# A fused attention and gated-MLP block: the start-up stage regrouped, with stacks copied from on-chip tiles, early row maxima, and token stores last

## Chip, cores and metric

The kernel runs on one core of a Trainium2 chip. The metric is the device time of one execution in microseconds (us); the median of several runs is given. All arithmetic is in float32, with matmul operands split into a high and a low part ("hi" and "lo") and multiplied in three products, so that precision is kept.

## What is computed

```python
# S = 2048 tokens, D = 512, H = 32 heads of 16, gated MLP of width 2 x 896
xn  = layernorm(x)
qkv = xn @ wqkv
p   = softmax(q @ k.T * 16 ** -0.5)          # per head, 2048 x 2048
A   = concat_heads(p @ v) @ wo
z   = gelu(xn @ w_in); z1, z2 = z[:, :896], layernorm(z[:, 896:])
B   = (z1 * (w_sp @ z2 + b_sp[:, None])) @ w_out
out = x + A + B
```

## The kernel before

Heads are taken in 16 pairs. For a pair p the "stacks" `qst[p % 2]` and `kst[p % 2]` hold, for each of its two heads at partitions 0 and 64, 48 rows: the 16 rows of q (or k) three times, as hi or lo parts in the order that makes one 48-row matmul give all three products. Two more rows carry the negated row maxima for the softmax (in `qst`) and ones (in `kst`).

The program has two stages.

The **prologue** (the body of `tc.manual_schedule`, L972 to L1022) is an order written out by hand. The tokens come in four groups g of 512. Per group: `norm_x` (statistics on VectorE, the scaling on ScalarE, L305), `turn_x` (16 TensorE transposes into four PSUM banks, each split into hi and lo by ScalarE and VectorE through `split`, L327 and L229), `qk_first` (24 matmuls by the weights `w0` of the first four pairs' q and k, L389, with a split and the stores to the DRAM scratch `qscr[0]`, `kscr[0]`), `load_stacks` (reads the stacks of pair 0 back from that scratch, L785) and `v_tile` (12 matmuls for one of the 16 tiles of v; `EARLY` = 4 of them are made here, L441). PSUM has four tiles, `dps` and three `sl`, taken in turn by `bank`. At the end the 16 transposed token tiles `xnT[g, c]` are put out to `xscr` (L1012) through `store`, which in the prologue issues on GpSimd's queue (L153).

The **steady stage** (the loop from L1229) writes out the rest of the program, with a planner that keeps a planned time for each engine and chooses, slot after slot, what TensorE does next. Its order of slots is fixed when the program is built. The slots are S (`scores`, L1076: one 512 x 128 piece of scores for two heads, followed by an exponential on ScalarE), M (`maxima`, L1093: the same product the other way round, followed by a maximum over 512 keys on VectorE, L806), V (`values`, L1170: eight exponentials times v, 32 matmuls in a burst), D (`dense_slot`, L1142: two matmuls of everything else, in the order v_rest, qk_rest, z2_all, z1_all, spatial, mlp_out, attn_out) and fillers (L1155). A "round" ends with a V burst; there are 128 of them. The first score needs the maxima of 512 queries over all keys: 16 M slots, then `max_fin` (L811), which writes the maxima to the scratch `mscr` and reads them back into the two extra rows of `qst`; both transfers go through SyncE's queue (SP), as do the loads of the next weights (`begin`, L249, under `weight`, L271). The planner lets M slots begin at planned time `FIRST` after the prologue (L1109).

In the built program each transfer on SP waits at its issue, among other things, for the one eight transfers earlier on SP to have landed.

Of the kernel before, what the change touches and what calls it, by code (L numbers as in the profile page):

```python
# [16 lines left out]
P = 128  # L17
# [13 lines left out]
GC = 0.7978845608028654  # L31
RING = 19
EARLY = 4
FIRST = 7.0
DEEP = 4
LEAD = 30
AGE = 6.0
# [14 lines left out]
def fused_block(ctx, tc, x, wqkv, wo, w_in, w_spT, b_sp, w_out, out):  # L52
# [96 lines left out]
    def store(dst, src, us=0.3):  # L149
        if steady:  # L150
            after(us, move, dst, src)
        else:
            nc.gpsimd.dma_start(raw(dst), raw(src))  # L153
# [63 lines left out]
    def t512(nm):  # L217
        return big.tile([P, 512], F32, tag="t512", name=nm, bufs=4)

    def hilo(nm):  # L220
        return big.tile([P, 2, 512], F32R, tag="hilo", name=nm, bufs=3)

    turns = [0]

    def bank():
        turns[0] += 1
        return (dps, *sl)[turns[0] % 4][:, 0, :]

    def split(dst_h, dst_l, src):  # L229
        act(dst_h, src, AF.Copy)  # L230
# [64 lines left out]
    def load_x(g):  # L295
        xt = [at_.tile([P, 2, D], F32, tag="pf", name=f"x{g}_{i}", bufs=PF) for i in (0, 2)]
        for i in range(len(xt)):
            k = 4 // len(xt)
            t = 4 * g + k * i
            rows = x[t * P:(t + k) * P, :]  # L300
            move(xt[i], rows if k == 1 else rows.rearrange("(a p) d -> p a d", p=P))
            for j in range(k):
                xs[g, k * i + j] = xt[i] if k == 1 else xt[i][:, j, :]

    def norm_x(g, parts=1):  # L305


        mv = sm.tile([P, 4, 2], F32, tag="mv", name=f"mv{g}", bufs=2)
        rs = sm.tile([P, 2, 4], F32, tag="rs", name=f"rs{g}", bufs=2)
        k = 4 // parts  # L310
        for a in range(parts):
            tiles = range(a * k, (a + 1) * k)
            sl = slice(a * k, (a + 1) * k)
            for i in tiles:
                st = sm.tile([P, 6], F32, tag="bst", name=f"bst{g}_{i}", bufs=4)
                nc.vector.bn_stats(st, xs[g, i])
                nc.vector.bn_aggr(mv[:, i, :], st)
            yield
            nc.scalar.activation(rs[:, 0, sl], mv[:, sl, 1], AF.Sqrt, bias=epst)
            nc.vector.reciprocal(rs[:, 0, sl], rs[:, 0, sl])  # L320
            nc.vector.scalar_tensor_tensor(rs[:, 1, sl], mv[:, sl, 0], -1.0, rs[:, 0, sl], ALU.mult, ALU.mult)
            for i in tiles:
                if i % 4 == 2:
                    yield
                nc.scalar.activation(xs[g, i], xs[g, i], AF.Identity, bias=rs[:, 1, i:i + 1], scale=rs[:, 0, i:i + 1])

    def turn_x(g):  # L327
        for c in range(ND):
            pt = bank()
            for i in range(4):  # L330
                nc.tensor.transpose(pt[:, i * P:(i + 1) * P], xs[g, i][:, c * P:(c + 1) * P], ident)
            t = piece(f"xnT{g}_{c}")
            split(t[:, 0, :], t[:, 1, :], pt)
            xnT[g, c] = t
# [43 lines left out]
    def qk_store(scr, order, hl, sl_, first=False):  # L378
        put = move if first else store
        r = 1 if order[0] == order[1] else 0  # L380
        put(scr[:, r:r + 2, sl_], hl)
        put(scr[:, 2 - 2 * r, sl_], hl[:, 0, :])

    def qk_weights(m, a):
        return f"wqk{m}_{a}", wqkv[:, a * D + m * P: a * D + (m + 1) * P], D, ND

    QK = ((0, 1, 0), (0, 0, 1))

    def qk_first(g, w):  # L389
        for a in range(2):  # L390
            acc = bank()
            for c in range(ND):
                t = xnT[g, c]
                mm3(acc, w[a][:, 0, c * P:(c + 1) * P], w[a][:, 1, c * P:(c + 1) * P], t[:, 0, :], t[:, 1, :], c == 0, c == ND - 1)
            hl = hilo(f"qkhl0_{a}_{g}")
            split(hl[:, 0, :], hl[:, 1, :], acc)
            qk_store((qscr, kscr)[a][0], QK[a], hl, slice(g * 512, (g + 1) * 512), True)
            yield

    def qk_out(m, g, a):  # L400
# [40 lines left out]
    def v_tile(t, ws):  # L441
        acc = bank()
        sl_ = slice((t % 4) * P, (t % 4 + 1) * P)
        for c in range(ND):
            xt = xnT[t // 4, c]
            mm3(acc, xt[:, 0, sl_], xt[:, 1, sl_], ws[c][:, 0, :], ws[c][:, 1, :], c == 0, c == ND - 1)
        act(vhead[:, t, :, :DH], acc.rearrange("p (h d) -> p h d", d=DH), AF.Copy)
# [337 lines left out]
    def load_stacks(p, cols=slice(0, S)):  # L785
        m, r = p // 4, (p % 4) * 2
        q, k = qst[p % 2], kst[p % 2]
        sl = [slice((r + j) * DH, (r + j + 1) * DH) for j in range(2)]
        for j in range(2):
            for i, (t, scr) in enumerate(((q, qscr), (k, kscr))):  # L790
                args = t[64 * j:64 * j + KS, cols], scr[m][sl[j], :, cols]
                if p and 2 * j + i:
                    later(2 * j + i, move, *args)
                else:
                    move(*args)

    NSTEP = NP * 64
    mmax = {}
    maxready = {}

    def max_red(i, k, ready):
        g, (t, kc) = i // 16, divmod(i % 16, 4)
        yield "D", td(1024)
        if i % 16 == 0:
            mmax[g] = at_.tile([P, 2, 4, 4], F32, tag="mm", name=f"mm{g}", bufs=2)
        nc.vector.tensor_reduce(mmax[g][:, :, t, kc], sl[k], AX.X, ALU.max)  # L806
        free_slot(k)
        if i % 16 == 15:
            yield from max_fin(g)
# [161 lines left out]
    with tc.manual_schedule(engines=engines):  # L971
        load_x(0)  # L972
        w0 = [piece(f"wqk0_{a}") for a in range(2)]
        w0r = [begin(*qk_weights(0, a), early=w0[a]) for a in range(2)]
        load_x(1)
        ones = t512("ones")
        nc.vector.memset(ones[0:32, 0:P], 1.0)
        wv, wvr = [], []
# [15 lines left out]
        init_rows(0)  # L994
        for r, t in zip(wvr, wv):
            end(r, t, True)
        norm = norm_x(1, 2)
        for g in range(NG):
            for _ in qk_first(g, w0):
                if g == 0:  # L1000
                    next(norm, 0)
            load_stacks(0, slice(g * 512, (g + 1) * 512))
            for t in range(EARLY * g // NG, EARLY * (g + 1) // NG):
                v_tile(t, wv)
            if g + 1 < NG:
                for _ in norm:
                    pass
                turn_x(g + 1)
                if g + 2 < NG:
                    norm = norm_x(g + 2)  # L1010
                    next(norm)
        for g in range(NG):  # L1012
            for c in range(ND):
                store(xscr[g][c], xnT[g, c])
        steady.append(True)
        braw = t512("braw")[0:16, 0:P]
        bhl = hilo("bhl")[0:16, :, 0:P]
        move(braw, b_sp)
        nc.vector.tensor_copy(bhl[:, 0, :], braw)
        nc.vector.tensor_sub(bhl[:, 1, :], braw, bhl[:, 0, :].bitcast(F32))  # L1020
        for a in range(2):
            move(bsplit[a:a + 1, :], bhl[:, a, :])  # L1022
        T.update(P=0.0, A=0.0, D=0.0, G=0.0)
        room["big"] = RING - 16 + EARLY
        prepare(wq, [((m, a), *qk_weights(m, a)) for m in (1, 2, 3) for a in range(2)])
# [16 lines left out]
        wrote = [0] * 3  # L1042
        stpos = {}
        mode = "R"
        n_st = n_mx = n_pv = 0

        def take(what, n=1):
            nonlocal pe, seen
# [44 lines left out]
        def maxima():  # L1093
            nonlocal n_mx
            p, r = divmod(n_mx, 64)
            tt, kc = divmod(r, 4)
            turn_to("R")
            k = take("m")
            for j in range(2):
                rows = slice(64 * j, 64 * j + KS)  # L1100
                nc.tensor.matmul(sl[k][:, j, :], qst[p % 2][rows, tt * P:(tt + 1) * P], kst[p % 2][rows, kc * 512:(kc + 1) * 512], start=True, stop=True)  # L1101
            T["P"] += SLOT
            spawn(max_red(n_mx, k, 0), 1, T["P"] + 0.22)
            n_mx += 1
# [7 lines left out]
        def has_dense(t):  # L1112
            nonlocal blocked, swap, hold, seen
            while not slots:
                if blocked > t or dfree[0] > t or hold or not queue:
                    return False
                it = next(queue[0], None)
                if it is None:
                    queue.pop(0)
                elif it[0] == "t":  # L1120
                    slots.extend(it[1])
                elif it[0] == "w":
                    blocked = t + it[1]
                elif it[0] == "s":
                    swap = True
                elif it[0] == "q":
                    hold = spent > 11 and n_pv < N
                elif it[0] == "e":
                    dfree[0] = FAR
                    held[0] = len(it[1])  # L1130
                    for g in it[1]:
                        spawn(g, 0, T["P"] + 0.25)
            if swap and seen < lastd:
                nc.tensor.drain()
                seen = pe
                T["P"] += DRAIN
            swap = False
            return True
# [156 lines left out]
```

## Time and profile before

| | us |
|---|---|
| timed runs | 1898.93, 1893.89, 1898.62 (median 1898.62) |
| profiled execution, its own time | 1894.84 |
| span of its trace | 1892.8 |
| TensorE busy in the span | 1829.1 (97%) |
| VectorE busy | 1443.6 (76%) |
| ScalarE busy | 1225.3 (65%) |
| GpSimd busy | 659.0 (35%) |

The profiled execution is one run; its own time is 2.04 us above the span of its trace. In the rows of the timeline the first column is the start and the second the length in us; a bracket at the end gives the engine's idle time before the row and what ended it. PEld rows are weight loads, which lie beside the matmuls.

### The profile page before, as it was taken

What the parts mean: (1) busy time and instruction counts of PE and PEld (TensorE: products, weight loads), DVE (VectorE), ACT (ScalarE), POOL (GpSimd) and SP (SyncE); (2) the same over time, 40 slices, a digit from 0 to 9 for tenths busy, and PEclk for the clock granted to TensorE, in tenths of its full rate; (3) what the DMA queues carried; (4) which work ended last, traced back from release to release, by engine and by line L of the source; (5) the groups of instructions that cost most, each with busy time, mean ns of one, the idle gap of its engine ahead of it and who ended that gap; (6) DMA issues with size and microseconds to landing.
All of it is one profiled execution on the core that took longest, in us unless ns stands there. A gap on an engine that the chain in (4) does not pass through costs nothing.

```text
span 1892.8 us, 38090 instructions
## 1 busy us (share of the span) xinstructions
PE 1829.1 (97%) x14830; PEld 1113.3 (59%) x14830; DVE 1443.6 (76%) x1677; ACT 1225.3 (65%) x1338; POOL 659.0 (35%) x757
## 2 busy tenths in 40 slices
PE   6899999999999999999999999999999999999998
PEld 5666566565555566566655666566565655555654
DVE  5578878888886878777877777787687778777883
ACT  4247777888775777666656666666566666565655
POOL 2302142787887777700161206000612030002110
PEclk9999999999998999999999999999999999999999
DMA  9506572444555354645677557463957666366342
GB/s 328 207 3 190 191 239 86 115 119 117 155 156 164 118 135 130 147 134 135 168 204 177 166 136 219 132 145 101 229 155 172 165 184 161 103 149 185 115 127 93
DMA packets 234732, 291.46 MB, mean 154 GB/s; under 512 B 36008, under 2 KB 136040, under 8 KB 231672
## 3 DMA queue, kind: packets, MB, share of 16 engines
q1 hardware_dynamic: 230328, 279.00, 54.2%
q0 software_dynamic: 4224, 10.04, 1.5%
q8 instruction: 116, 1.90, 0.5%
q14 instruction: 64, 0.52, 0.1%
HBM read 186.98 MB, written 101.98 MB: 153 GB/s over the span
## 4 chain that ended last, share of the span: by engine, by line
PE 83%; DMA 6%; DVE 4%; POOL 3%; issue 2%; ACT 2%; SPq 0%; DVEq 0%; POOLq 0%; ACTq 0%
PE dps L1146 33%; PE sl L1184 22%; PE sl L1087 13%; PE sl L1101 12%; DVE mm L806 3%; DMA zs<-z2scr 2%; PE dps L1160 1%; POOL wsp L282 1%; ACT pf L69 1%; DMA wsp_11r<-in_w_spT 1%; DMA qst<-qscr 1%; DMA wqk<-in_wqkv 1%; DMA xnT__6256<-xscr 1%; POOL wsp L280 1%; DMA hscr<-hhl 0%
## 5 line engine op out<-in xcount | busy, mean ns | idle before, releaser
L806 DVE TENSOR_REDUCE mm<-sl 128x2 f32<-128x1024 f32 x1024 | 1226.4, 1223 | 190.6 <-PE sl L1101 186.4
L69 ACT ACTIVATE pf<-sl 128x1024 f32<-128x1024 f32 x1024 | 1043.3, 1026 | 369.9 <-PE sl L1087 330.9
L1184 PE MATMUL sl<-pf,vall 128*32 128x512 f32 x4096 | 467.8, 597 | 1.3 <-ACT pf L69 1.3
L1146 PE MATMUL dps<-wsp,zs 64*128 64x512 f32 x2688 | 449.2, 396 | 8.6 <-DMA zs<-z2scr 8.5
L1087 PE MATMUL sl<-qst,kst 50*128 50x512 f32 x2048 | 445.2, 421 | 12.2 <-DVE mm L806 2.9
L1101 PE MATMUL sl<-kst,qst 48*128 48x512 f32 x2048 | 432.6, 409 | 6.4 <-DVE mm L806 3.2
L1087 PEld LDWEIGHTS sl<-qst,kst 50*128 50x128 f32 x2048 | 200.5, 185 | 221.7 <-issue 85.7
L1146 PEld LDWEIGHTS dps<-wsp,zs 64*128 64x128 f32 x2688 | 272.8, 189 | 51.4 <-DMA zs<-z2scr 8.1
L1184 PEld LDWEIGHTS sl<-pf,vall 128*32 128x32 f32 x4096 | 120.3, 110 | 272.5 <-issue 240.8
L1101 PEld LDWEIGHTS sl<-kst,qst 48*128 48x128 f32 x2048 | 200.4, 186 | 110.8 <-ACT pf L69 54.1
L1204 DVE TENSOR_TENSOR e<-sl,e 128x512 f32<-128x512 f32 x64 | 44.1, 690 | 165.4 <-PE sl L1184 134.5
L718 POOL TENSOR_TENSOR hhl<-z1i,hhl 128x512 fp32r<-128x512 f32 x28 | 35.5, 1284 | 353.0 <-ACT hhl L69 303.3
L69 ACT ACTIVATE e<-sl 128x512 f32<-128x512 f32 x64 | 38.4, 600 | 172.9 <-PE sl L1184 158.3
L1146 PE MATMUL dps<-w,xt 64*128 64x448 f32 x768 | 110.8, 369 | 2.3 <-ACT z L69 0.4
L1146 PE MATMUL dps<-wout,hp 64*128 64x512 f32 x672 | 111.4, 392 | 0.0
L1146 PEld LDWEIGHTS dps<-w,xt 64*128 64x128 f32 x768 | 73.7, 186 | 17.4 <-issue 8.0
L1146 PEld LDWEIGHTS dps<-wout,hp 64*128 64x128 f32 x672 | 65.5, 187 | 8.9
L418 POOL TENSOR_TENSOR qkhl<-qr,qkhl 128x512 fp32r<-128x512 f32 x24 | 30.4, 1285 | 114.9 <-ACT qkhl L69 114.8
L853 POOL TENSOR_TENSOR ob<-ob 128x512 f32<-128x512 f32 (+1 forms) x16 | 20.6, 1286 | 141.1 <-DMA ob<-rscr 108.6
L849 POOL TENSOR_TENSOR ob<-ob 128x512 f32<-128x512 f32 (+1 forms) x16 | 20.5, 1284 | 129.4 <-DMA ob<-escr 129.4
L1146 PE MATMUL dps<-xnT,wqk 64*128 64x512 f32 x288 | 47.4, 396 | 1.1 <-ACT vall L69 0.4
L1160 PE MATMUL dps<-brow,zeror 64*128 64x512 f32 x258 | 46.5, 402 | 1.7 <-ACT z L69 1.4
(277 smaller groups left out, 1595.0 us busy)
## 6 DMA issues: line engine op xcount, KB each, us to landing
zs<-z2scr SPq DMA_DIRECT2D x192, 256.0 KB
escr<-e SPq DMA_DIRECT2D x60, 256.0 KB
hscr<-hhl SPq DMA_DIRECT2D x28, 512.0 KB
qst<-qscr SPq DMA_DIRECT2D x30, 384.0 KB
kst<-kscr SPq DMA_DIRECT2D x30, 384.0 KB
xscr<-xnT POOLq DMA_DIRECT2D x16, 512.0 KB, 4.6
qscr<-qkhl SPq DMA_DIRECT2D x16, 512.0 KB
kscr<-qkhl SPq DMA_DIRECT2D x16, 512.0 KB
```

What stands on the lines that cost most here:

```text
L69: return nc.scalar.activation(out, in_, func, **kw)
L418: nc.gpsimd.tensor_sub(hl[:, 1, :], raw_, hl[:, 0, :].bitcast(F32))
L718: nc.gpsimd.tensor_sub(hl[:, 1, :], z1, hl[:, 0, :].bitcast(F32))
L806: nc.vector.tensor_reduce(mmax[g][:, :, t, kc], sl[k], AX.X, ALU.max)
L849: nc.gpsimd.tensor_add(both_[rows, 0, :], both_[rows, 0, :], both_[rows, 1, :])
L853: nc.gpsimd.tensor_mul(both_[rows, 0, :], both_[rows, 0, :], both_[rows, 1, :])
L1087: nc.tensor.matmul(sl[k][:, j, :], kst[p % 2][rows, kt * P:(kt + 1) * P], qst[p % 2][rows, c * 512:(c + 1) * 512], start=True, stop=True)
L1101: nc.tensor.matmul(sl[k][:, j, :], qst[p % 2][rows, tt * P:(tt + 1) * P], kst[p % 2][rows, kc * 512:(kc + 1) * 512], start=True, stop=True)
L1146: nc.tensor.matmul(dps[:, bank, :w], lhs, rhs, start=go, stop=stop)
L1160: nc.tensor.matmul(dps[:, bank, :], zeror[r:r + 64], brow[r:r + 64], start=not begun, stop=not begun)
L1184: nc.tensor.matmul(sl[k][cols:cols + VW, 0, :], vpack(kt + r, 2 * p + j), pf[:, j * 512:(j + 1) * 512], start=n == n_pv, stop=n == n_pv + ...
L1204: nc.vector.tensor_add(e, sl[k][:, 0, :], e)
```

## The change

The changed prologue does five things.

- Tokens are normed and turned a group ahead: group 1 is normed and turned before the projections of group 0, and group g + 2 beside those of group g.
- `qk_first` copies the stacks of pair 0 straight from the split tile with six transfers of 16 rows for each of q (on SP) and k (on GpSimd's queue); `load_stacks(0, ...)` is gone. The scratch stores stay.
- `first_maxima(kc)` makes the first 512 queries' maxima over one quarter of the keys, four M products with their four reductions, after `qk_first` of the following group. Twelve of the first sixteen M products are thus in the prologue; the loop begins with `n_mx` = 12, and the first sixteen go by quarters of the keys.
- The 16 token stores go out through `move`, that is on SP, after everything else of the prologue; the loads and splits of `b_sp` come early.
- The loop's M slots may begin at planned time 3.0 (it was 7.0), and the D queue isn't held at its "q" marks until all tiles of v are made.

```diff
-FIRST = 7.0
+FIRST = 3.0
...
+    def turn4():
+        turns[0] += 1
+        return turns[0] % 4
+
     def bank():
-        turns[0] += 1
-        return (dps, *sl)[turns[0] % 4][:, 0, :]
+        return (dps, *sl)[turn4()][:, 0, :]
...
+    mmax = {}
     QK = ((0, 1, 0), (0, 0, 1))
+    PARTS = QK
+
+    def first_maxima(kc):
+
+        for t in range(4):
+            acc = (dps, *sl)[turn4()]
+            for j in range(2):
+                rows = slice(64 * j, 64 * j + KS)
+                nc.tensor.matmul(acc[:, j, :], qst[0][rows, t * P:(t + 1) * P], kst[0][rows, kc * 512:(kc + 1) * 512], start=True, stop=True)
+            if 0 not in mmax:
+                mmax[0] = at_.tile([P, 2, 4, 4], F32, tag="mm", name="mm0", bufs=2)
+            nc.vector.tensor_reduce(mmax[0][:, :, t, kc], acc, AX.X, ALU.max)
...
             split(hl[:, 0, :], hl[:, 1, :], acc)
-            qk_store((qscr, kscr)[a][0], QK[a], hl, slice(g * 512, (g + 1) * 512), True)
+            cols = slice(g * 512, (g + 1) * 512)
+            put = (nc.sync, nc.gpsimd)[a]
+            for j in range(2):
+                for i, part in enumerate(PARTS[a]):
+                    row = 64 * j + i * DH
+                    put.dma_start((qst, kst)[a][0][row:row + DH, cols].bitcast(F32), hl[j * DH:(j + 1) * DH, part, :].bitcast(F32))
+            qk_store((qscr, kscr)[a][0], QK[a], hl, cols, True)
             yield
...
     def max_red(i, k, ready):
-        g, (t, kc) = i // 16, divmod(i % 16, 4)
+        g, (t, kc) = i // 16, divmod(i % 16, 4) if i >= 16 else (i % 4, i // 4)
...
-        if i % 16 == 0:
+        if i and i % 16 == 0:
...
         load_x(1)
+        braw = t512("braw")[0:16, 0:P]
+        bhl = hilo("bhl")[0:16, :, 0:P]
+        move(braw, b_sp)
...
-        norm = norm_x(1, 2)
-        for g in range(NG):
-            for _ in qk_first(g, w0):
-                if g == 0:
-                    next(norm, 0)
-            load_stacks(0, slice(g * 512, (g + 1) * 512))
-            for t in range(EARLY * g // NG, EARLY * (g + 1) // NG):
-                v_tile(t, wv)
-            if g + 1 < NG:
-                for _ in norm:
-                    pass
-                turn_x(g + 1)
-                if g + 2 < NG:
-                    norm = norm_x(g + 2)
-                    next(norm)
-        for g in range(NG):
-            for c in range(ND):
-                store(xscr[g][c], xnT[g, c])
-        steady.append(True)
-        braw = t512("braw")[0:16, 0:P]
-        bhl = hilo("bhl")[0:16, :, 0:P]
-        move(braw, b_sp)
+        run(norm_x(1, 2))
         nc.vector.tensor_copy(bhl[:, 0, :], braw)
         nc.vector.tensor_sub(bhl[:, 1, :], braw, bhl[:, 0, :].bitcast(F32))
         for a in range(2):
             move(bsplit[a:a + 1, :], bhl[:, a, :])
+        turn_x(1)
+        for g in range(NG):
+            if g + 2 < NG:
+                norm = norm_x(g + 2)
+                next(norm)
+            for _ in qk_first(g, w0):
+                if g + 2 < NG:
+                    next(norm, 0)
+            if g + 2 < NG:
+                run(norm)
+            if g:
+                first_maxima(g - 1)
+            for t in range(EARLY * g // NG, EARLY * (g + 1) // NG):
+                v_tile(t, wv)
+            if g + 2 < NG:
+                turn_x(g + 2)
+        for g in range(NG):
+            for c in range(ND):
+                move(xscr[g][c], xnT[g, c])
+        steady.append(True)
...
-        n_st = n_mx = n_pv = 0
+        n_st, n_mx, n_pv = 0, 12, 0
...
-            tt, kc = divmod(r, 4)
+            tt, kc = divmod(r, 4) if n_mx >= 16 else (r % 4, r // 4)
...
-                    hold = spent > 11 and n_pv < N
+                    hold = spent > 11 and n_pv < N and len(vdone) == NT - EARLY
```

More of the change, by code (lines that the diff above doesn't have):

```diff
@@ L797, in fused_block @@
     NSTEP = NP * 64
-    mmax = {}
     maxready = {}
     def max_red(i, k, ready):
-        g, (t, kc) = i // 16, divmod(i % 16, 4)
+        g, (t, kc) = i // 16, divmod(i % 16, 4) if i >= 16 else (i % 4, i // 4)
         yield "D", td(1024)
-        if i % 16 == 0:
+        if i and i % 16 == 0:
             mmax[g] = at_.tile([P, 2, 4, 4], F32, tag="mm", name=f"mm{g}", bufs=2)
```

## The prediction

> **What bounds the kernel now.** I read the page first, then busy time by stage, then the timeline of the first 110 us and of the end.
>
> ```profile
> span 1892.8 us, 38090 instructions
> PE 1829.1 (97%) x14830; PEld 1113.3 (59%) x14830; DVE 1443.6 (76%) x1677; ACT 1225.3 (65%) x1338; POOL 659.0 (35%) x757
> ...
> 0.00:72.00 72.00, 52.24 (x208) 40.66 (x208) 35.02 (x81) 30.67 (x51) 17.25 (x37) 0.93 0.91 318
> 72.00:110.00 38.00, 34.85 (x280) 26.53 (x282) 30.71 (x33) 5.69 (x10) 11.12 (x12) 1.00 0.22 66
> ...
> 1850.00:1892.80 42.80, 35.81 (x314) 19.11 (x312) 13.31 (x14) 19.74 (x22) 0.00 (x0) 0.97 0.24 87
> ```
>
> TensorE is busy 97% of the time; of its 64 us of idle time 20 lie in the first 72 us (72.00 - 52.24) and 7 in the last 43. Its work is fixed, and the D slots that are not done early are done later at full price. So the end moves by what TensorE's idle time moves. Starting the scores earlier is worth nothing by itself: what counts is how many slots TensorE has behind it when the first score goes. The next view is L1146 (D slots, two matmuls each) and L1101 (M) alone in the same second window.
>
> ```profile
> 72.00:110.00 38.00, 31.62 (x226) 21.53 (x228) 1.00 0.22 66
> 72.00:110.00 38.00, 9.63 (x52) 5.12 (x52) 1.00 0.22 66
> ...
> 81.14 0.87 PE L1146 MATMUL dps<-kst,xnT 64*128 64x512 f32 x6
> 81.85 0.40 PE L1101 MATMUL sl<-kst,qst 48*128 48x512 f32 x2
> 82.09 0.86 PE L1146 MATMUL dps<-kst,xnT 64*128 64x512 f32 x6
> ...
> 98.92 0.34 SPq L123 DMA_DIRECT2D mscr<-ms  x1
> 100.42 1.42 SPq L123 DMA_DIRECT2D qst<-mscr  x2
> 109.89 0.41 PE L1087 MATMUL sl<-qst,kst 50*128 50x512 f32 x2
> ```
>
> Before the first score (109.89) stand 113 D and 26 M slots. Three D slots take 0.71 us (81.14 to 81.85) and an M slot 0.24, so a slot of either kind is 0.237. In the changed program's instruction order the first score has 57 D slots ahead of it and 14 M slots in the loop, besides the 12 in the prologue. The maxima come out even (26 and 26); 56 D slots, 56 x 0.237 = 13.3 us, are still owed when the first score starts. Fillers go from 129 slots to 127 (-0.5 us). So the first score must go 12.8 us sooner than 109.89 for the change to break even, but for the tail (below).
>
> **The prologue.** The rows are those of group 0's norm and projections, of VectorE's weight splits, and of a later group.
>
> ```profile
> 4.69 0.69 DVE L316 BATCH_NORM_STATS2 bst<-x 128x6 f32<-128x512 f32 x1 [2.65 <-DMA x<-in_x]
> 9.50 1.52 ACT L325 ACTIVATE x<-x,rs 128x512 f32<-128x512 f32 x2 [0.43 <-DVE rs L321]
> 13.04 1.06 PE L331 MATMUL dps<-ident,x 128*128 128x128 f32 x4
> 14.94 0.79 PE L234 MATMUL sl<-xnT,wqk 128*128 128x512 f32 x1 [0.83 <-DVE xnT L231]
> 19.25 0.69 DVE L257 TENSOR_TENSOR kst<-wv3r,kst 128x512 fp32r<-128x512 f32 x1 [0.77 <-DMA kst<-in_wqkv]
> 25.34 0.39 PE L236 MATMUL sl<-kst,xnT 128*128 128x512 f32 x1
> 30.60 0.80 PE L234 MATMUL dps<-xnT,wqk 128*128 128x512 f32 x1
> 41.69 2.93 ACT L325 ACTIVATE x<-x,rs 128x512 f32<-128x512 f32 x4 [0.44 <-DVE rs L321]
> 42.56 0.33 PE L331 MATMUL sl<-ident,x 128*128 128x128 f32 x1 [2.13 <-ACT x L325]
> 47.29 0.48 PE L234 MATMUL sl<-xnT,wqk 128*128 128x512 f32 x1
> 52.84 0.39 PE L234 MATMUL sl<-qst,xnT 128*128 128x512 f32 x1
> 55.34 0.39 PE L236 MATMUL sl<-kst,xnT 128*128 128x512 f32 x1
> 57.85 0.33 PE L331 MATMUL sl<-ident,x 128*128 128x128 f32 x1 [2.13 <-ACT x L325]
> 61.84 0.77 PE L234 MATMUL sl<-xnT,wqk 128*128 128x512 f32 x1
> 66.07 0.60 ACT L69 ACTIVATE qkhl<-sl 128x512 fp32r<-128x512 f32 x1 [3.25 <-PE sl L236]
> 66.70 0.69 DVE L231 TENSOR_TENSOR qkhl<-sl,qkhl 128x512 fp32r<-128x512 f32 x1 [3.15 <-ACT qkhl L69]
> 72.12 1.65 PE L1146 MATMUL dps<-qst,xnT 64*128 64x512 f32 x12 [0.69 <-ACT vall L69]
> 79.65 12.53 DVE L806 TENSOR_REDUCE mm<-sl 128x2 f32<-128x1024 f32 x11
> ```
>
> Until 14.1 (13.04 + 1.06) both kernels are alike. Now TensorE starts the projections of group 0 at 14.94. In the new order group 1's 16 transposes stand ahead of them, and these wait for group 1's norm, which on VectorE stands behind the four splits of the v weights, done at 19.94 (19.25 + 0.69). A norm takes 6.33 (4.69 to 11.02), so the last tile is scaled at 26.3; transposes and the first split take 2.7 to 3 (44.62 to 47.29, after the row of 41.69). The projections of group 0 start at 29.3, 14.4 later than now.
>
> After that the new order gains. Projections and v tile take 10.8 in group 0 (14.94 to 25.73), where the first twelve matmuls run at half speed, and 5.55 + 2.9 in a later group (47.29, 52.84, 55.73). Group 0 ends at 40.1; group 2's tiles are scaled by then, its transposes take 1.9, and group 1 starts at 42.1: the 2.1 us stall of the row of 42.56 and the slow transposes behind it are gone. Group 1's projections end at 47.65. Here comes the new wait: the fourth M product takes the bank of the second projection, whose copy on ScalarE stands behind two scalings of group 3 (1.5), which stand behind VectorE's statistics; its split ends at 51.0, the first reduction, 1.14 long (12.53 / 11), at 52.2, and only then the v tile gets its bank. TensorE has one M product to do between 47.9 and 52.2. After today's gap of 2.13 (row of 57.85) twelve projections took 4.23 (61.84 to 66.07), where 2.8 is normal (half of 5.55): a gap costs 1.4 in slow matmuls. So the v tile ends at 56.5 and group 2 starts, after 1.9 of transposes, at 58.5. Groups 2 and 3 have no transposes after them but the same chain: projections 5.55, split 1.35 (66.07 to 67.39), one reduction 1.15, v tile 2.9, together 11.0; the gap is 1.8, shorter than any that I have a row for, and I add half of 1.4. Group 3 starts at 70.2, its v tile ends at 81.9, and with ScalarE's copy (0.69, the row of 72.12) the loop starts at 82.6, 10.5 later than 72.12.
>
> Of these 10.5, the 12 M slots are only 2.8 of TensorE's work. The row of 14.94 stands for slow matmuls in group 0, and the new order leaves TensorE without work from 14.1 to 22.4. The Trainium skill ("TensorE: Matmul & The Clock Gate", Part 1) says that TensorE's clock is halved after an idle window of about 3.4 us and restored after about 3.4 us of work. The row of 57.85 differs: a gap of 2.13 was enough, with sparse transposes behind it. By the skill only eight of group 0's matmuls would run slow and the gaps of groups 2 and 3 would cost nothing, and the sum would be 2.2 lower; by the trace it stays.
>
> **The token stores on SP.** Today they go out on GpSimd's queue as each group is ready, beside other traffic.
>
> ```profile
> 20.00:25.00 5.00, 5.00 (x23) 4.10 (x23) 3.53 (x9) 1.71 (x4) 3.75 (x8) 1.00 1.05 393
> 21.60 2.15 POOL L153 DMA_DIRECT2D xscr<-xnT  x4
> 24.39 1.77 SPq L123 DMA_DIRECT2D kscr<-qkhl  x2
> 33.49 0.30 SPq L123 DMA_DIRECT2D kst<-kscr  x1
> ...
> xscr<-xnT POOLq DMA_DIRECT2D x16, 512.0 KB, 4.6
> ```
>
> In the new order 16 x 512 KB go out on SP from 77.1, when group 3's k is split; five loads of weights follow, and only then the store of the first maxima, which waits by semaphore for the 14th token store. The transfer engines were full at 393 GB/s. The last store of k (0.79 MB), the tokens (8.39) and the five loads (1.31), 10.5 MB, take 26.9 us at 390: until 104.0. That such a queue delays what is behind it shows in the rows of 24.39 and 33.49: the read of `kscr` could go only 7.3 us after its store was issued. The maxima themselves are ready early, about 10 us after the loop's start (26 D matmuls 3.1, five reductions 5.7, `max_fin` 0.9), at 92.3. Their store lands 1.5 after the queue is through (98.92 to 100.42), at 105.5; the way back costs the same and a sixth load of weights (0.26 MB, 0.7): 107.7. TensorE's own way there is 71 slots, 16.8 us, and two waits of 0.7 for ScalarE's copies (the bracket of 72.12): it would be at the first score at 100.8 and stands still for 6.9. That is the price that the change pays: the cover of the token stores is gone just when a small, urgent transfer needs the queue. Bounds: nothing if small transfers pass by (the round trip then ends at 95.3); 12 if the weights' 512-byte rows move at half the rate and SP's issue adds some.
>
> The removed reads of the stacks and the early `b_sp` cost nothing: the rows `qst`, `kst` of a group are needed 10 us after its split. GpSimd's 24 new issues take 0.54 each (2.15 / 4), 3.2 a group, with nothing urgent behind them.
>
> **The tail.** The D queue runs 48 slots later against the rounds, so that the last two tiles of attn_out lie where fillers are now.
>
> ```profile
> 1876.78 3.64 PE L1184 MATMUL sl<-pf,vall 128*32 128x512 f32 x32
> 1880.35 1.14 PE L943 MATMUL sl<-sel,on 32*128 32x512 f32 x8
> 1881.99 2.12 PE L1160 MATMUL dps<-brow,zeror 64*128 64x512 f32 x16
> 1885.20 1.14 PE L943 MATMUL sl<-sel,on 32*128 32x512 f32 x8 [1.09 <-DVE on L936]
> ```
>
> After the last V burst 24 D slots (5.7) take the place of eight fillers (2.1) and the 1.1 of idle: 2.5 later. In the round before it 24 D slots replace 11 fillers in a round that waits for ScalarE anyway; I count 1.7 instead of 3.1. Idle time cut in the tail: 1.1 + 1.3 = 2.4.
>
> **The sum.** First score at 107.7 instead of 109.9: -2.2. Owed: 54 slots net of fillers, +12.8. Tail -2.4. Together +8.2: span 1901.0 and, with the 2.04 around it, 1903.0 against the profiled execution's 1894.84. The median of the timed runs lies 3.8 above that execution, near the upper two of three; on it the forecast is 1906.8. 0.3% (5.7 us) is about what a measurement of this kernel can tell from no change.
>
> **The rivals.** (1) The maxima are not held up, because the token stores drain before or beside them. Then the first score goes at 100.8 and the sum is 8.2 - 6.9 = +1.3: 1899.9, no change, on the other side of the forecast. It decides if the store of `mscr` lands by 98. For it: the mean DMA share of 0.22 in 72 to 110 leaves the engines free. Against: the wait for the 14th token store is in the program. Chance 0.2. (2) The prologue is also quicker than my chain: with the loop at 75 (reductions and splits overlap better than I string them, and the clock holds) 7.6 less than (1): -6.3, 1892.3, faster. The gaps of 2.13 that go speak for it, the 29.3 of group 0 against it. Chance 0.17. (3) Both go worse: every new gap costs the full 1.4 (1.4 more) and the queue the 12 (5.1 more): +14.7, 1913.3. Chance 0.13. Forecast 0.5.
>
> **How the numbers follow.** The forecast's own spread is 4 either way, 1903 to 1911; some four fifths of it lie above 0.3%. Slower: 0.4 of it and rival 3, 0.54. Faster: rival 2 but for a part that stays within the bound, and a little of rival 1, 0.16. Within 0.3%: the rest, 0.30. The range from 1893 to 1914 takes in rival 1, the forecast, the lower half of rival 3 and the edge of rival 2.
>
> **What would show it.** Right: group 0's first projection near 29, the loop's first D matmul near 82, `mscr` issued only after 95 and the first score's matmul near 108 behind a wait for a DMA. Wrong: no such wait (rival 1), or the loop's start before 76 (rival 2).

## The result: slower by 0.86%, and the profile after

The changed kernel takes 1911.91 us (median of four runs, 1910.16 to 1913.99) where the kernel before takes 1898.3 (median of four). The ratio is 1.0086, interval 1.0067 to 1.0104. The two medians stand 13.6 us apart. The profiled execution has a time of its own of 1910.16 and a span of 1908.4, which is 15.6 above the span before; the accounts below are of these two executions. The kernel before has itself taken between 1890.24 and 1901.77 in the runs on record, so a difference of two executions is not known to better than a few us. The forecast had the direction, the place and the cause of the stall; the price was 8.2 and is 15.6 (13.6 by the medians).

The page of the changed kernel:

```profile
span 1908.4 us, 38143 instructions
PE 1824.5 (96%) x14826; PEld 1104.8 (58%) x14826; DVE 1442.9 (76%) x1677; ACT 1223.6 (64%) x1338; POOL 661.6 (35%) x765
```

Busy time by stage, with the same columns as before (granted clock, share of the transfer engines and GB/s at the end):

```profile
0.00:72.00 72.00, 46.61 (x206) 36.16 (x207) 43.17 (x90) 29.38 (x49) 17.32 (x39) 0.88 0.60 186
82.00:110.00 28.00, 16.34 (x128) 12.06 (x124) 16.57 (x19) 3.46 (x5) 4.26 (x6) 0.86 0.96 357
```

TensorE is busy for 4.6 us less than before, and the span is 15.6 longer: idle time has grown by 20. In the stretch from 82 to 110 TensorE works 16.34 of 28 us while the transfer engines are at 0.96: the place of the loss. The waits of the changed kernel's TensorE name it (us in total, times, longest):

```profile
PE sl L1110 <- DMA qst<-mscr: 11.8, 2, 11.4
```

Its timeline shows how that wait comes about:

```profile
78.33 21.13 SPq L123 DMA_DIRECT2D xscr<-xnT  x16
90.21 0.21 DVE L844 STREAM_TRANSPOSE ms<-mrow 128x32 f32<-128x32 f32 x1
104.53 0.87 SPq L123 DMA_DIRECT2D mscr<-ms  x1
109.00 1.43 SPq L123 DMA_DIRECT2D qst<-mscr  x2
111.11 1.43 PE L1110 MATMUL sl<-qst,kst 50*128 50x512 f32 x2 [11.40 <-DMA qst<-mscr]
...
119.18 1.13 PE L1169 MATMUL dps<-kst,xnT 64*128 64x512 f32 x8
120.14 0.40 PE L1110 MATMUL sl<-qst,kst 50*128 50x512 f32 x2
```

The maxima are ready at 90.4. Their store is issued 14 us later, at 104.53, behind the 16 token stores and the weights on SP, and is read back from 109.00 on. TensorE has nothing left from 99.7 and stands still for 11.4 us. What follows the stall is seen in its busy time in short stretches, where the number after the busy times is the granted clock:

```profile
110.90:114.50 3.60, 3.31 (x12) 1.95 (x14) 0.00 (x0) 1.02 (x1) 3.52 (x4) 0.50 0.01 1
114.50:117.00 2.50, 2.50 (x14) 1.99 (x12) 1.23 (x1) 1.02 (x1) 2.22 (x3) 0.50 0.00 0
117.00:119.00 2.00, 2.00 (x12) 1.58 (x10) 1.23 (x1) 0.43 (x1) 0.00 (x0) 0.50 0.00 0
119.00:121.00 2.00, 2.00 (x18) 1.46 (x16) 1.33 (x2) 1.01 (x2) 0.00 (x0) 0.94 0.00 0
```

For 8 us after the stall TensorE is busy, at half its clock. Between 111.11 and 120.14 it does 20 slots (40 matmuls) in 9.03 us; at 0.237 they would take 4.74. That is 4.3 us that the sum did not have. (In experiment 2 below, without the stall, the same 20 slots take 5.0 us, from 98.87 to 103.88, which makes it 4.0.)

The V burst that closes the third round stands at the same work in both kernels, but for the D slots still owed, and so do the last two bursts. Their rows in the timeline of the kernel before:

```profile
152.30 1.07 PE L1184 MATMUL sl<-pf,vall 128*32 128x512 f32 x8
1866.16 3.64 PE L1184 MATMUL sl<-pf,vall 128*32 128x512 f32 x32
1876.78 3.64 PE L1184 MATMUL sl<-pf,vall 128*32 128x512 f32 x32
```

And in that of the changed kernel:

```profile
165.82 1.50 PE L1207 MATMUL sl<-pf,vall 128*32 128x512 f32 x12
1877.37 3.64 PE L1207 MATMUL sl<-pf,vall 128*32 128x512 f32 x32
1889.44 3.64 PE L1207 MATMUL sl<-pf,vall 128*32 128x512 f32 x32
```

13.5 us are lost by the third burst already. They are the first score, +1.2 (111.11 against 109.89); the slow matmuls, +4.3; and 32 D slots that the changed order does between the first score and this burst where the order before did them ahead of the first score (111 against 79), 32 x 0.237 = 7.6. Together 13.1. The other 2.1 come by the end. On the way the distance wanders (+4.4 at a burst near 590 us, +11.2 at the last but one). At 590 us it is small because the kernel before loses time there itself: its granted clock is 0.50 in the windows from 563 to 572 and from 587 to 593, where the changed kernel's is 1.00.

### The profile page after: what moved, and what is told of

Read it like the earlier page. It is cut to its first block, busy times and chain, and to the rows that moved or that the text cites. A ratio compares the mean times of both kernels' runs of the same rounds, so it can differ in the third digit from the quotient of the medians.

```text
span 1908.4 us, 38143 instructions
## 1 busy us (share of the span) xinstructions
PE 1824.5 (96%) x14826; PEld 1104.8 (58%) x14826; DVE 1442.9 (76%) x1677; ACT 1223.6 (64%) x1338; POOL 661.6 (35%) x765
## 4 chain that ended last, share of the span: by engine, by line
PE 79%; DMA 6%; POOL 6%; DVE 4%; issue 3%; SPq 2%; ACT 1%; DVEq 0%; POOLq 0%; ACTq 0%
PE dps L1169 32%; PE sl L1207 21%; PE sl L1110 13%; PE sl L1124 11%; DVE mm L827 3%; SPq L123 2%; POOL wsp L285 1%; DMA zs<-z2scr 1%; PE dps L1183 1%; DMA kst<-in_wqkv 1%; POOL wsp L283 1%; DMA wsp_10r<-in_w_spT 1%; DMA w_6r<-in_w_in 1%; ACT pf L69 0%; POOL z2hl L545 0%
## 5 line engine op out<-in xcount | busy, mean ns | idle before, releaser
L827 DVE TENSOR_REDUCE mm<-sl 128x2 f32<-128x1024 f32 x1012 | 1210.9, 1223 | 215.2 <-PE sl L1124 209.4
L1169 PE MATMUL dps<-wsp,zs 64*128 64x512 f32 x2688 | 446.1, 395 | 13.7 <-DMA zs<-z2scr 13.7
L1124 PE MATMUL sl<-kst,qst 48*128 48x512 f32 x2024 | 425.9, 409 | 8.6 <-DVE mm L827 4.2
L1124 PEld LDWEIGHTS sl<-kst,qst 48*128 48x128 f32 x2024 | 196.5, 186 | 115.5 <-ACT pf L69 56.1
```

Source lines behind the costliest of these rows:

```text
L1169: nc.tensor.matmul(dps[:, bank, :w], lhs, rhs, start=go, stop=stop)
```

## The experiments

Two theories had to be told apart first: that the loss lies in the moment of the token stores, or that it lies in their queue. Then came the slow clock, the order of the prologue, the early maxima and `FIRST`. All kernels compute the same thing; the third has extra matmuls that add nothing. Each ratio is to the kernel before, timed beside the experiment (medians of 1896.1 to 1896.5); the rows are of one execution each. In what follows "third burst" is the V burst that closes the third round: 152.30 before, 165.82 in the changed kernel.

**1. The same stores at the same moment, on GpSimd's queue** (against the changed kernel).

```diff
-                move(xscr[g][c], xnT[g, c])
+                store(xscr[g][c], xnT[g, c])
```

> The changed kernel with one edit: the 16 token stores stay at the end of the prologue but go out on GpSimd's queue instead of SP's. Theory Q (the queue): the store of the first maxima no longer stands behind 8.4 MB on SP. It is issued when the loads ahead of it allow, about 95, and lands about 3 us later, so the first score goes near 101 instead of 111.1; TensorE's wait shrinks from 11.4 to 1 or 2, the slow matmuls after it (4.3 us) go too, and the time falls by some 13 to 15, to about 1898. Rival M (the moment): the transfer engines are full then whichever queue is used, so the round trip is as late as before, near 109, and the time stays within 3 of 1911.9.

Measured: 1907.07 us, 1.0058 [1.0036, 1.0080] of the kernel before. Its timeline:

```profile
93.07 5.67 SPq L123 DMA_DIRECT2D mscr<-ms  x1
107.40 1.44 SPq L123 DMA_DIRECT2D qst<-mscr  x2
109.73 1.30 PE L1110 MATMUL sl<-qst,kst 50*128 50x512 f32 x2 [11.79 <-DMA qst<-mscr]
```

The rate of its transfers, in 40 slices of 1 us from 72 to 112:

```profile
GB/s 41 66 162 266 328 232 369 393 391 352 381 400 409 396 417 397 412 411 410 399 422 401 401 410 392 407 410 406 413 408 384 325 279 155 64 13 2 6 0 0
```

The store of the maxima is now issued at 93.07, with no token store ahead of it on SP, and is nevertheless not back before 107.40. That is when the transfer engines have run dry (155 and 64 GB/s in the slices from 105 to 107). So another queue for the token stores does not help (the time is 4.8 under the changed kernel's median, the span 3.1). What it does to the other queue shows in the queues' shares from 84 to 102 us (q0 is GpSimd's, q1 is SP's; packets, MB, share of the engines):

```profile
q0 software_dynamic: 1761, 6.41, 87.6%
q1 hardware_dynamic: 1761, 0.88, 16.3%
```

Both queues move the same number of packets, but those of the weights' loads on SP are mostly of 512 bytes and those of the token stores mostly of 4096. So SP's queue gets 49 GB/s beside GpSimd's 356, and on it the store of the maxima is in line behind five loads of weights: its packets start at 103.58, when most of theirs have started. Whether 16 KB with no load ahead of them on SP would have passed beside the token stores was not run.

**2. The same stores on GpSimd's queue, each group as soon as it is turned** (against the changed kernel).

```diff
             xnT[g, c] = t
+        for c in range(ND):
+            nc.gpsimd.dma_start(raw(xscr[g][c]), raw(xnT[g, c]))
...
-        for g in range(NG):
-            for c in range(ND):
-                move(xscr[g][c], xnT[g, c])
```

> The changed kernel with one edit: each group's four token stores go out on GpSimd's queue as soon as the group is turned, as they do in the kernel before. Q and M agree: the stores are hidden under the prologue, the first score goes near 99, no wait of over 1 us stands before it, and the time falls by the stall (11.4) and the slow matmuls after it (4.3), to about 1896, 2 under the kernel before. Rival O (the slots owed): the stall only moves waiting about, because the D slots owed and the later tail set the end; then no more than half of it comes back, and the time stays above 1903.

Measured: 1893.46 us, 0.9987 [0.9974, 0.9999]. Its timeline:

```profile
89.79 0.34 SPq L123 DMA_DIRECT2D mscr<-ms  x1
91.28 1.43 SPq L123 DMA_DIRECT2D qst<-mscr  x2
98.87 0.40 PE L1109 MATMUL sl<-qst,kst 50*128 50x512 f32 x2
149.53 3.64 PE L1206 MATMUL sl<-pf,vall 128*32 128x512 f32 x32
```

The store lands after 1.5 us again, the first score is at 98.87 without a wait, and the third burst comes 16.3 earlier than in the changed kernel: 12.2 of stall and 4.1 of slow matmuls. The whole loss is thus the moment of the token stores. Without it the rest of the change is a gain of some 2 us, just clear of the noise.

**3. Work for TensorE in the stall** (against the changed kernel): 44 filler slots, products with zeros, ahead of the first score.

```diff
+            if n_st == 0:
+                for _ in range(44):
+                    for r, bank in zip((0, 64), (halves if begun else (0, 1))):
+                        nc.tensor.matmul(dps[:, bank, :], zeror[r:r + 64], brow[r:r + 64], start=not begun, stop=not begun)
```

> The changed kernel with one edit: 44 filler slots (zero products, about 10.4 us) right before the first score, in the time in which TensorE otherwise stands still. Theory: the matmuls from 111 to 120 run at half speed because TensorE stood still, and cost 4.3 us; with the fillers they run at full speed at once and the time falls by 3 to 4.5, to about 1908. Rival: they are slow because of something that comes with the first score (the exponentials' table, the reductions, full transfer engines); then the rows after the first score stay at 0.43 apart and the time stays at 1912 or rises by what the fillers stick out.

Measured: 1906.17 us, 1.0051 [1.0035, 1.0067]. Its timeline:

```profile
98.53 10.18 PE L1105 MATMUL dps<-brow,zeror 64*128 64x512 f32 x88
110.25 1.06 PE L1114 MATMUL sl<-qst,kst 50*128 50x512 f32 x2 [1.54 <-DMA qst<-mscr]
161.66 3.64 PE L1211 MATMUL sl<-pf,vall 128*32 128x512 f32 x32
```

The first score is 0.9 earlier than in the changed kernel and the third burst 4.2 earlier: with the stall filled, 3.3 us are saved behind it. From 110 to 115 us the granted clock is 1.00 here. The clock after the stall is a cost of its own, as the windows had it; the fall of 5.7 between the medians is somewhat more than the 3 to 4.5 expected.

**4. The kernel before, with its token stores put where the change puts them** (against the kernel before).

```diff
-                store(xscr[g][c], xnT[g, c])
+                move(xscr[g][c], xnT[g, c])
```

> The kernel before with one part of the change alone: its 16 token stores go out at the end of the prologue on SP instead of GpSimd's queue. Theory: the stores hold SP from about 75 to 97, the weights' loads land near 100 and the store of the first maxima, ready at 98.9, waits for the fifth and sixth of them, which wait for GpSimd; the first score moves from 109.9 to 112 to 115 and the time rises by 2 to 6, to 1900 to 1904. Rival: 27 us between the prologue's end and the first maxima are cover enough, and the time stays at 1898.

Measured: 1919.87 us, 1.0118 [1.0092, 1.0145], far from what was expected. The stall lay elsewhere, as its timeline shows:

```profile
96.04 1.19 SPq L123 DMA_DIRECT2D braw<-in_b_sp  x1
101.65 0.21 DVE L1019 CAST bhl<-braw 16x128 fp32r<-16x128 f32 x1 [28.86 <-DMA braw<-in_b_sp]
103.37 0.80 PE L1101 MATMUL sl<-kst,qst 48*128 48x512 f32 x2 [19.86 <-DVE mm L806]
123.83 0.34 SPq L123 DMA_DIRECT2D mscr<-ms  x1
```

In the kernel before the load of `b_sp` stands behind the stores, now also on SP. VectorE's first instruction on it waits 28.86 us, all the reductions of maxima stand behind that on VectorE, and TensorE stands still for 19.86 in its M slots. So the "early `b_sp`", which the prediction costed at nothing, is what lets the token stores stand last at all.

**5. The same with `b_sp` early** (against experiment 4).

```diff
         load_x(1)
+        braw = t512("braw")[0:16, 0:P]
+        bhl = hilo("bhl")[0:16, :, 0:P]
+        move(braw, b_sp)
...
+        nc.vector.tensor_copy(bhl[:, 0, :], braw)
+        nc.vector.tensor_sub(bhl[:, 1, :], braw, bhl[:, 0, :].bitcast(F32))
+        for a in range(2):
+            move(bsplit[a:a + 1, :], bhl[:, a, :])
         norm = norm_x(1, 2)
...
         steady.append(True)
-        braw = t512("braw")[0:16, 0:P]
...
```

> The kernel before with two parts of the change: the token stores last on SP, and b_sp loaded and split early, so that VectorE no longer waits for it behind the stores. If the 24.9 us of the stores alone were VectorE's wait for b_sp, most of them go: the maxima are ready near 99 as in the kernel before, and what is left is the store of the maxima behind the fifth and sixth load of weights (about 108) and slow matmuls after TensorE's wait, 8 to 14 us: 1905 to 1911. Rival: nothing is left, because 27 us are cover enough: 1897.

Measured: 1896.1 us, 0.9995 [0.9982, 1.0008]. Its timeline:

```profile
100.79 0.64 SPq L123 DMA_DIRECT2D mscr<-ms  x1
104.86 1.45 SPq L123 DMA_DIRECT2D qst<-mscr  x2
110.55 0.41 PE L1087 MATMUL sl<-qst,kst 50*128 50x512 f32 x2
```

The expected 1905 to 1911 did not come; its rival did. Here too the store needs 4.1 us to land, and with a way back as long as the changed kernel's (2.1) the maxima are there near 107. But TensorE has 113 D and 26 M slots of cover and arrives at 110.55. The same stores at the same place, the end of the prologue, cost nothing in the old order and some 16 us (by the third burst) in the new one, which has 57 D and 14 M slots.

**6. `FIRST` back at 7.0** (against experiment 2), which puts 15 more D slots ahead of the first score.

```diff
-FIRST = 3.0
+FIRST = 7.0
```

> The changed kernel with the token stores early and FIRST at 7.0 as before: 15 more D slots stand ahead of the first score. Accounts of slots: the first score goes 3.5 later and 3.5 less is owed: 1893.5 give or take 1.5. Rival (an early first score is worth its time): up by 3.5, 1897.

Measured: 1891.62 us, 0.9976 [0.9965, 0.9988]. Its timeline:

```profile
102.43 0.41 PE L1109 MATMUL sl<-qst,kst 50*128 50x512 f32 x2
```

The first score is 3.6 later than in experiment 2 (15 x 0.237), and the third burst 0.4 earlier than in experiment 2. Slots moved across the first score cost nothing and bring nothing, as the account of owed slots says.

**7. Without the early maxima** (against experiment 2): no `first_maxima`, all M slots in the loop.

```diff
-        if i and i % 16 == 0:
+        if i % 16 == 0:
...
-            if g:
-                first_maxima(g - 1)
...
-        n_st, n_mx, n_pv = 0, 12, 0
+        n_st, n_mx, n_pv = 0, 0, 0
```

> The changed kernel with the token stores early, and without the twelve maxima in the prologue: all 16 are made in the loop, from planned time 3. By the accounts of slots, the first score then has 96 D slots ahead of it instead of 57 (39 x 0.237 = 9.2 us less owed) and goes some 7 us later, near 106, because the prologue no longer waits for its reductions: the time falls by 1 to 3 against the early stores alone, to about 1891.5; the early maxima were worth nothing. Rival: the early first score is what the change gains by (ScalarE and VectorE start sooner); then the time rises by 5 or more, to 1898 or above.

Measured: 1890.39 us, 0.9966 [0.9954, 0.9979]. Its timeline:

```profile
103.01 0.43 PE L1107 MATMUL sl<-qst,kst 50*128 50x512 f32 x2
145.44 3.64 PE L1204 MATMUL sl<-pf,vall 128*32 128x512 f32 x32
```

The third burst is 4.1 earlier than in experiment 2, with the same work done. The early products bring the first score forward (98.87 against 103.01) and cost TensorE more in waits for banks and reductions than they bring: experiment 2 has 5.1 us of such waits in its prologue, this one none. At the end 1.7 us of span are left of the 4.1, and 3.1 between the medians, whose intervals overlap a little.

**8. Projections first** (against experiment 2): the projections of group g again ahead of the turning of group g + 1.

```diff
-        run(norm_x(1, 2))
...
-        turn_x(1)
+        norm = norm_x(1, 2)
         for g in range(NG):
-            if g + 2 < NG:
-                norm = norm_x(g + 2)
-                next(norm)
             for _ in qk_first(g, w0):
-                if g + 2 < NG:
+                if g + 1 < NG:
                     next(norm, 0)
...
-            if g + 2 < NG:
-                turn_x(g + 2)
+            if g + 1 < NG:
+                turn_x(g + 1)
+                if g + 2 < NG:
+                    norm = norm_x(g + 2)
+                    next(norm)
```

> The changed kernel with the token stores early (as in the run before) and one more edit: each group is turned after the projections and v tile of the group ahead of it, with its norm spread over those projections, so that group 0's projections start at 15 and not at 29. Theory W: TensorE's wait for group 1's norm (10.2 us) is idle time that nothing gives back, so the loop starts near 71 instead of 80, the first score goes near 90 instead of 98.9, and the time falls by 8 to 10 against the early stores alone (1893.5), to about 1884.5, faster than both kernels. Rival: the norms now stand late again and each later group waits for them as in the kernel before (two waits of over 2 us and slow matmuls behind them); then 4 or less is left of it, 1889 or more.

Measured: 1888.01 us, 0.9959 [0.9945, 0.9973]. Its timeline:

```profile
15.26 0.50 PE L237 MATMUL sl<-xnT,wqk 128*128 128x512 f32 x1 [1.05 <-DVE xnT L234]
72.98 1.65 PE L1167 MATMUL dps<-qst,xnT 64*128 64x512 f32 x12 [0.69 <-ACT vall L69]
92.55 0.40 PE L1108 MATMUL sl<-qst,kst 50*128 50x512 f32 x2
```

The loop starts 6.3 earlier than in experiment 2 (72.98 against 79.32), the third burst comes 6.3 earlier (143.24), and the span is 3.7 shorter. The turning a group ahead costs 6 us in the prologue, less than the expectation had. By the medians the two differ by 5.4, between the 8 to 10 of the expectation and the 4 of its rival. Why the profiled executions differ by less at the end stays open: the distance is 5.7 near 920 us and 3.5 near 1410 us, and the loss in between is traced only in part. In these stretches TensorE's clock is granted at half for 17.1 us in this execution and for 13.7 in experiment 2's.

**9. Both: projections first, no early maxima, stores early** (against experiment 8; the edit is that of 7).

> The version with projections before the next group's turn and the token stores early on GpSimd's queue (1888.0 us), now also without the twelve early M products: the loop begins with none made, and all 26 go in the loop. Theory (TensorE's idle time is what counts; the early products only insert waits for a bank and a reduction, worth 3 us in the other order of the prologue): 1885 to 1887, first score near 97 with some 96 D slots ahead of it. Rival (the early products' waits are hidden in this order, since the next group's transposes lie behind them and have nothing to wait for): 1888 to 1889, no difference to the version with them.

Measured: 1885.07 us, 0.9935 [0.9918, 0.9951], the fastest of all. Its timeline:

```profile
65.00 2.93 PE L1165 MATMUL dps<-qst,xnT 64*128 64x512 f32 x12 [3.63 <-ACT vall L69]
100.28 0.43 PE L1106 MATMUL sl<-qst,kst 50*128 50x512 f32 x2
142.71 3.64 PE L1203 MATMUL sl<-pf,vall 128*32 128x512 f32 x32
```

Of the change this keeps the stacks copied from the split tile, the early `b_sp`, `FIRST` and the D queue's new rule. The loop starts at 65.00, 7.1 before that of the kernel before, though it begins with a wait of 3.63. The theory's 1885 to 1887 holds as a number; the first score is 3 later than it said. Its cause is not shown: the third burst is only 0.5 earlier than in experiment 8 (142.71 against 143.24), since the wait of 3.63 takes the place of most of the waits that went. Up to there the rival (the early products' waits are hidden in this order) is nearer. The rest of the 2.6 us of span comes after 530 us, and the intervals of experiments 8 and 9 overlap.

## Why the prediction was right about the stall and short in its price

**The loop's start: 82.6 forecast, 79.98 measured.** Rows of the changed kernel:

```profile
23.87 0.47 PE L334 MATMUL sl<-ident,x 128*128 128x128 f32 x1 [10.17 <-ACT x L328]
29.60 0.78 PE L237 MATMUL sl<-xnT,wqk 128*128 128x512 f32 x1
49.26 0.49 PE L400 MATMUL sl<-kst,qst 48*128 48x512 f32 x2 [2.03 <-DVE qkhl L234]
50.40 0.50 PE L237 MATMUL sl<-qst,xnT 128*128 128x512 f32 x1 [0.64 <-DVE mm L403]
64.11 0.50 PE L400 MATMUL dps<-kst,qst 48*128 48x512 f32 x2 [0.57 <-DVE qkhl L234]
65.24 0.50 PE L237 MATMUL sl<-qst,xnT 128*128 128x512 f32 x1 [0.63 <-DVE mm L403]
79.98 1.65 PE L1169 MATMUL dps<-qst,xnT 64*128 64x512 f32 x12 [0.69 <-ACT vall L69]
```

Group 0's projections at 29.3 (29.60 measured) and the wait for the fourth product's bank and reduction are there as told: 2.03 and 0.64 of idle time in group 1, 0.57 and 0.63 in group 2. Two sizes were too large. Group 0 takes 8.7 us from 29.60 to group 2's first transpose (38.30), not 10.8, because the slow phase had largely passed under the transposes from 23.87 on. And the short gaps of groups 2 and 3 cost no clock. The longer one of group 1 did: its v tile takes 4.4 us (50.40 to 54.84) where group 2's takes 2.8 (65.24 to 68.06), 1.6 more, and 1.4 was forecast. That size is in part luck: in experiments 1 and 3 gaps of the same length stand at the same place (2.02 and 0.63), and the granted clock from 50 to 55 us is 1.00 there against 0.66 here. By the prediction's estimate from the Trainium skill ("TensorE: Matmul & The Clock Gate", Part 1) the sum would have been 2.2 lower, a start at 80.4. On the short gaps the trace agrees with it, and on group 0 in direction (the estimate has eight slow matmuls, the trace two, from 29.60 to 30.56); a gap of 2.03 with a second of 0.64 behind it was nevertheless enough to slow the clock in this execution.

**The token stores: first score forecast at 107.7, measured at 111.11.** This is the first term that was mis-sized. The mechanism was right, `mscr` was issued at 104.53 ("only after 95"), and the maxima were ready before their forecast (90.4, not 92.3). That the 104.0 of the sum lies close to the issue is chance: it stands for the moment when the bytes are through. What failed is that moment, and with it the landing of the store 1.5 later, at 105.5. The rate of the changed kernel's transfers, in slices of 1 us from 72 to 112, shows it:

```profile
GB/s 23 43 55 57 232 289 266 234 375 422 414 410 426 401 438 406 397 426 406 426 406 418 406 406 410 397 410 410 410 374 225 285 302 312 298 277 90 0 4 4
```

The bytes are through at about 108.3 and not at 104.0: the stores were issued from 78.33 on, not from 77.1, and the loads behind them move at some 300 GB/s, not at 390. The store took 4.5 us and came back 0.7 after the engines had run dry. The way back, 2.2 in the forecast, took 2.1. With the loop's earlier start TensorE arrived earlier as well, at 99.7, so that 11.4 us of stall stand where 6.9 were forecast, inside the bounds of 0 to 12. Rival 1, no hold-up, is refuted by the wait's row; the reason given against it (the wait for the 14th token store) was not the whole one, since in experiment 1, without that wait, the maxima came back only 1.6 earlier.

**The clock after the stall.** This is the step that failed outright, a term that the prediction put at nothing without a reason: 4.3 us by the windows, 3.3 to 4.1 by experiments 3 and 2. "Its work is fixed" holds for the number of slots, not for their time. The prediction charged 1.4 for a gap of 2.13 and then nothing for a stall of 6.9. Had the stall been charged at that row alone, the sum would have been 9.6.

**The owed slots and the tail.** They fit, as what remains when the rest is taken off. Of the 15.6, 1.2 are the first score and 4.3 the slow clock; 10.1 remain for 54 slots and the tail, and 12.8 - 2.4 = 10.4 were forecast. Experiment 2, which has the same slots without the stall, agrees within its noise: its first score is 11.0 earlier than before, which with the 10.4 makes -0.6, and its ratio stands for -2.5 (-4.9 to -0.2). From the last V burst to the end the change adds 2.9 (18.96 against 16.02; forecast 2.5), and in the round before it 1.5 (12.07 against 10.62; forecast 1.7). Experiment 6 confirms the price of a slot.

The miss of 7.4 is thus 3.4 (first score), 4.3 (clock) and -0.3 (slots and tail). By the medians the miss is 5.1 (1911.91 against 1906.8), so that one of its parts is smaller than in this pair of executions; the runs do not say which. Rival 2 did not come. With the hold-up taken away, experiment 2 is faster than before, but by 2.7 us of span and not 6.3, because its loop starts at 79.32 and not at 75. Rival 3's 1913.3 lies nearest to the result, by half of its mechanism and by luck: the stall of 11.4 is close to its 12, but its dearer gaps did not come, and the slow clock, which it does not have, stands in their place. For the removed reads of the stacks "nothing" stands: no wait of TensorE names the copies that replace them, though no run tested them alone. Early `b_sp` costs nothing either, and it is what keeps the late stores from costing more still (experiments 4 and 5).

## What to carry to other kernels

Before bringing an urgent small transfer forward, ask what will be in flight then. Here it landed only when the bulk traffic had drained: behind it on its own queue, or behind loads that bulk stores on another queue slowed down. So bulk stores belong where enough other work covers the drain. Price a stall of TensorE as the wait plus the slow clock behind it. And an earlier start of the next stage is no gain by itself: the work that it skips is owed, and here the plain order (projections first, maxima in the loop, stores early) beat both the kernel before and the change.

## What the runs showed of the hardware that was not expected

A store of 16 KB that takes 1.5 us beside idle transfer engines (98.92 to 100.42, kernel before) took 4.5 us behind loads on its own queue (changed kernel), and 14.3 us behind such loads with 8 MB on another queue beside them (experiment 1, 93.07 to 107.40). The issue itself took 5.67 us there instead of 0.34. Two busy queues moved equal numbers of packets, not of bytes (1761 each from 84 to 102 us, 0.88 and 6.41 MB).

After the stall of 11.40 us the clock stayed at 0.50 through 8 us in which TensorE was busy for 7.8 of 8.1; the stretch of slow matmuls after the gaps of 2.03 and 0.64 in the prologue was over within 4 us. After stalls of 11.79 (experiment 1) and 19.86 us (experiment 4) the slow stretch was 7.1 and 5.0 us long, so it does not grow with the stall. The Trainium skill ("TensorE: Matmul & The Clock Gate", Part 1) gives about 3.4 us of work until the clock is restored; the row after the long stall shows more than twice that, and no run here says why. In the traces the moments at which the granted clock changes lie whole multiples of some 3.41 us apart (30.50, 50.98, 54.39, 102.18 and 119.25 in the changed kernel). That may be why equal gaps slow the clock in one execution and not in another, which was not tested.
